# Attention into a bilinear feed-forward layer: query transposes on VectorE, scores in 32-row tiles, folds over eight tiles, and two batches woven together at the start

## The chip, the cores and the metric

The kernel runs on one core of a Trainium2 chip. A core has a matrix engine (TensorE, PE in the profile, with its weight loads shown as PEld), a vector engine (VectorE, DVE), a scalar engine (ScalarE, ACT), GpSimd (POOL), which here mostly issues input transfers, and SyncE (SP), which here issues the output transfers. Each engine runs its own instructions in order; they wait for each other through semaphores. TensorE writes its results to PSUM, a small memory of eight banks per partition, from which VectorE or ScalarE copy them out ("eviction"). The metric is device time in microseconds, the median of several runs.

## The reference

Eight batches of eight heads, 576 positions, head size 64, 32 memory slots per head; then a bilinear feed-forward layer over the 4608 tokens (512 wide, 1536 hidden).

```python
a = np.exp(phi); a = a / a.sum(axis=2)                 # softmax over the 32 slots
k_m = np.einsum('bhsm,bhsd->bhmd', a, k)               # 32 x 64 per head
v_m = np.einsum('bhsm,bhsd->bhmd', a, v)
scores = (q @ k_m.T) / sqrt(64)
attn = softmax(scores, axis=-1)                        # over the 32 slots
x = concat_heads(attn @ v_m)                           # 4608 x 512
out = ((x @ w_a) * (x @ w_b)) @ w_out                  # 4608 x 512
```

## The kernel before

The kernel never forms `x`. For each batch the generator `attention(b)` does, in this order: the exponential of `phi` on ScalarE (`exp_sb`, two instructions); the sums over positions with keys and values (`pkv`, 72 small matmuls, four tiles of the array abreast), copied out as `kvm` with the reciprocals `rphi`; the queries turned by TensorE (`pqT`, 20 transposes) and copied out by VectorE (`qT`); the sums turned (`pT`, 8 transposes) and copied out by ScalarE (`kvT`); the scores (`pscore`, four groups of four matmuls) and their exponential `E` on ScalarE; the denominators (`pD`) with reciprocals `rD` on VectorE; those spread back over the slots (`pR`) and multiplied into `E`, which gives `A`; and the **fold**: the values times the weights, `pva`, in 12 groups of four matmuls, evicted alternately by ScalarE and VectorE into `vab`, the weights of the feed-forward layer for this batch. The weights come in three chunks of 512 columns (`load_wab(n)`), and the fold of chunk n needs chunk n.

`up(b, ...)` then makes the hidden layer of a batch in 12 steps. A step has two halves: four matmuls `pa` (two PSUM tiles of 288 columns, evicted by ScalarE as `a_sb`) and four `pb` (multiplied with `a_sb` by VectorE into `ht`). `down(c)` makes 128 output rows from 12 matmuls `po`, evicted by VectorE or ScalarE in turn (`o_sb`) and stored by SyncE.

The order of the instructions on each engine is the order in which the Python code issues them; there is no scheduler. After every half step `advance` issues a few matmuls of `down` ("work": 48 or 60 in a batch) and then a few yields of the attention of the next batch ("side", 40 spread over the 12 steps, of which the attention uses up 32 or so). The attention of batch 0 runs alone, ahead of the first step:

```python
gens = {b: attention(b) for b in range(1)}
for _ in gens[0]:
    pass
```

The pool `ps_at` has **two** PSUM buffers, taken in turn by everything in the attention (`pkv`, `pqT`, `pT`, `pscore`, `pD`, `pR`, `pva`); `ps_up` has two for `pa` and two for `pb`, `ps_dn` two for `po`. Input transfers stand in one queue on GpSimd, in the order of the calls: batch 0, weight chunk 0, chunks 1 and 2, batch 1, `w_out`, and then one batch per `up`.

Of the kernel before, what the change touches and what calls it, by code (L numbers as in the profile page):

```python
# [13 lines left out]
P = 128  # L14
CS = 16.0
# [3 lines left out]
def kernel(  # L19
# [54 lines left out]
    inputs = {}  # L74
    kv_sbs = [consts.tile([P, 3, NHP, NI * D], F16, name=f"kv_sb{t}") for t in range(2)]
    for t in range(2):
        nc.vector.memset(kv_sbs[t][:, 2], 8.0)

    def load_kv(b):
        phi_sb = inp.tile([P, NHP, NI * M], F32, name="phi_sb")  # L80
        nc.gpsimd.dma_start(out=phi_sb, in_=rows(phi, b))  # L81
        kv_sb = kv_sbs[b % 2]
        nc.gpsimd.dma_start(out=kv_sb[:, 0], in_=rows(k, b))
        nc.gpsimd.dma_start(out=kv_sb[:, 1], in_=rows(v, b))
        inputs[b] = [phi_sb, kv_sb]

    def load_q(b):
        q_sb = inp.tile([P, NHP, NI * D], F16, name="q_sb")
        nc.gpsimd.dma_start(out=q_sb, in_=rows(q, b))
        inputs[b].append(q_sb)  # L90
# [10 lines left out]
    load_kv(0)  # L101
    load_q(0)
# [12 lines left out]
    spread = consts.tile([P, P], F16, name="spread")  # L115
    nc.vector.memset(spread, 0.0)
    for t in range(4):
        nc.gpsimd.affine_select(out=spread, in_=spread, compare_op=ALU.not_equal, fill=8.0 * CS,
                                base=-32 * t, pattern=[[-8, 4], [0, 32]], channel_multiplier=1)
    load_wab(1)  # L120
    load_wab(2)
    load_kv(1)
    load_q(1)
# [6 lines left out]
    def attention(b):  # L130
        phi_sb, kv_sb, q_sb = inputs.pop(b)
        exp_sb = mid.tile([P, NHP, NI, M], F16, name="exp_sb")
        for z in range(2):
            nc.scalar.activation(  # L134
                out=exp_sb[:, 2 * z:2 * z + 2, :, :],
                in_=phi_sb[:, 2 * z:2 * z + 2, :].rearrange("p c (i m) -> p c i m", m=M),
                func=AF.Exp,
            )
            yield

        qT = mid.tile([P, NHP, 5, P], F16, name="qT")
        kvm = mid.tile([P, 2, P], F16, name="kvm")
        kvT = mid.tile([P, 2, 2, P], F16, name="kvT")
        rphi = small.tile([P, 2], F32, name="rphi")

        def transposes(hps, cs):
            t = ps_at.tile([P, len(hps), len(cs), P], F16, name="pqT", tag="at")
            w = min(P, NI * D - P * cs[0])
            for x, hp in enumerate(hps):
                for y, c in enumerate(cs):  # L150
                    nc.tensor.transpose(out=t[:w, x, y, :], in_=q_sb[:, hp, P * c:P * c + w], identity=ident)  # L151
            return t

        pkv = ps_at.tile([P, 2, 3 * D], F32, name="pkv", tag="at")
        for g in range(2):
            for i in range(NI):
                for j in range(4):
                    r, hp = j % 2, 2 * g + j // 2
                    nc.tensor.matmul(  # L159
                        pkv[32 * j:32 * j + 32, g, :],  # L160
                        exp_sb[64 * r:64 * r + 64, hp, i, :],
                        kv_sb[64 * r:64 * r + 64, :, hp, D * i:D * (i + 1)],
                        start=(i == 0),
                        stop=(i == NI - 1),
                        tile_position=(64 * r, 32 * j),
                    )
                if i in (4,):
                    yield
            if g == 0:
                yield  # L170
        nc.vector.tensor_copy(out=kvm, in_=pkv[:, :, 0:2 * D])
        nc.vector.reciprocal(out=rphi, in_=pkv[:, :, 2 * D])
        yield

        for hps, cs in (((0, 1), (0, 1, 2, 3)), ((2, 3), (0, 1, 2, 3)), ((0, 1, 2, 3), (4,))):
            t = transposes(hps, cs)
            w = 64 if cs[0] == 4 else P
            nc.vector.tensor_copy(out=qT[:w, hps[0]:hps[-1] + 1, cs[0]:cs[-1] + 1, :], in_=t[:w])
            yield

        pT = ps_at.tile([P, 2, 2, P], F16, name="pT", tag="at")
        for g in range(2):
            for x in range(2):
                for z in range(2):
                    nc.tensor.transpose(out=pT[64 * z:64 * z + 64, g, x, :], in_=kvm[:, g, D * x:D * (x + 1)],
                                        identity=ident, tile_position=(0, 64 * z))
        nc.scalar.copy(out=kvT, in_=pT)
        yield

        E = mid.tile([P, 2, 640], F16, name="E")  # L190
        Ev = E.rearrange("p g (c two s) -> p g c two s", two=2, s=64)
        for g in range(2):
            for par in range(2):
                n = 5 - par
                ps = ps_at.tile([P, 5, 64], F32, name="pscore", tag="at")
                for j in range(4):
                    h = 4 * g + j
                    nc.tensor.matmul(  # L198
                        ps[32 * j:32 * j + 32, 0:n, :],
                        kvT[64 * par:64 * par + 64, g, 0, M * j:M * j + M],  # L200
                        qT[64 * par:64 * par + 64, h // 2, 0:n, 64 * (h % 2):64 * (h % 2) + 64],
                        start=True,
                        stop=True,
                        tile_position=(64 * par, 32 * j),
                    )
                nc.scalar.activation(out=Ev[:, g, 0:n, par, :], in_=ps[:, 0:n, :], func=AF.Exp,  # L206
                                     scale=rphi[:, g:g + 1])
                yield

        pD = ps_at.tile([P, HALF], F32, name="pD", tag="at")  # L210
        for g in range(2):
            for hf in range(2):
                t = 2 * g + hf
                nc.tensor.matmul(pD[32 * t:32 * t + 32, :], sel, E[:, g, HALF * hf:HALF * (hf + 1)],  # L214
                                 start=True, stop=True, tile_position=(0, 32 * t))
        rD = mid.tile([P, HALF], F16, name="rD")
        for z in range(2):
            sl = slice(z * HALF // 2, (z + 1) * HALF // 2)
            with nc.allow_low_precision("softmax denominators"):
                nc.vector.reciprocal(out=rD[:, sl], in_=pD[:, sl])  # L220
        yield

        A = mid.tile([P, 2, S], F16, name="A")
        for g in range(2):
            for hf in range(2):
                t = 2 * g + hf
                pR = ps_at.tile([P, HALF], F32, name="pR", tag="at")
                nc.tensor.matmul(pR, spread[32 * t:32 * t + 32, :], rD[32 * t:32 * t + 32, :],  # L228
                                 start=True, stop=True, tile_position=(32 * t, 0))
                sl = slice(HALF * hf, HALF * (hf + 1))  # L230
                nc.vector.scalar_tensor_tensor(out=A[:, g, sl], in0=E[:, g, sl], scalar=rphi[:, g:g + 1],  # L231
                                               in1=pR, op0=ALU.mult, op1=ALU.mult)
                yield
        attn[b] = A

        vab = [mid.tile([P, 2, d_ff], F16, name=f"vab{z}") for z in range(2)]
        vabs[b] = vab
        e = 0
        for n in range(NCH):
            for z in range(2):  # L240
                for g in range(2):
                    pva = ps_at.tile([P, 512], F32, name="pva", tag="at")
                    for j in range(4):
                        r, hp = j % 2, 2 * g + j // 2
                        nc.tensor.matmul(  # L245
                            pva[32 * j:32 * j + 32, :],
                            kvT[64 * r:64 * r + 64, g, 1, M * j:M * j + M],
                            w_sbs[z][64 * r:64 * r + 64, hp, 512 * n:512 * (n + 1)],
                            start=True,
                            stop=True,  # L250
                            tile_position=(64 * r, 32 * j),
                        )
                    dst = vab[z][:, g, 512 * n:512 * (n + 1)]
                    if e % 2:
                        nc.vector.tensor_copy(out=dst, in_=pva)  # L255
                    else:
                        nc.scalar.copy(out=dst, in_=pva)  # L257
                    e += 1
                    yield
# [24 lines left out]
    def chain(gens):  # L284
        for g in gens:
            yield from g

    def pump(gen, n):
        for _ in range(n):
            if next(gen, "end") == "end":  # L290
                return False
        return True
# [92 lines left out]
```

## Time and profile before

| what | value |
|---|---|
| median of 3 runs | 322.86 us (321.48 to 323.45) |
| profiled execution | 323.5 us, of it span 321.8 us |
| PE busy | 285.2 us (89%) |
| DVE busy | 170.0 us (53%) |
| ACT busy | 131.3 us (41%) |
| first matmul | at 12.02 us |
| first step of `up(0)` | at 33.03 us |
| last `po` ends, then eviction and store | at 317.3 us |

Times in the trace count from the start of the span. A row of the timeline gives the start, the duration, engine, line, operation, result<-inputs and a count, and in brackets how long the engine was idle before it and who ended that wait. In the chain of work that ended last, a row gives the start, the time until the next piece, and the engine with its result; there a busy TensorE's groups add up to the elapsed time, so these are the rows from which a group's cost is read. A matmul's tile stands ahead of its shape: `64*32` uses 64 rows and 32 columns of the array, `128*128` all of it. The granted clock of TensorE stands in tenths of full speed on the page and as a fraction in the table by windows.

### The profile page before, as it was taken

What the parts mean: (1) busy time and instruction counts of PE and PEld (TensorE: products, weight loads), DVE (VectorE), ACT (ScalarE), POOL (GpSimd) and SP (SyncE); (2) the same over time, 40 slices, a digit from 0 to 9 for tenths busy, and PEclk for the clock granted to TensorE, in tenths of its full rate; (3) what the DMA queues carried; (4) which work ended last, traced back from release to release, by engine and by line L of the source; (5) the groups of instructions that cost most, each with busy time, mean ns of one, the idle gap of its engine ahead of it and who ended that gap; (6) DMA issues with size and microseconds to landing.
All of it is one profiled execution on the core that took longest, in us unless ns stands there. A gap on an engine that the chain in (4) does not pass through costs nothing.

```text
span 321.8 us, 6497 instructions
## 1 busy us (share of the span) xinstructions
PE 285.2 (89%) x2576; PEld 147.5 (46%) x2576; DVE 170.0 (53%) x350; ACT 131.3 (41%) x315; POOL 33.0 (10%) x53
## 2 busy tenths in 40 slices
PE   0438697999899989999899989999899989999994
PEld 0411352365336634455345634465346534566641
DVE  5145256755765466634675547544864565654410
ACT  3023433555364334445345253546264335344300
POOL 8522220002000300012000300000000000000000
PEclk9985587899999999999799999999999999999999
DMA  7999999948612692149512691111102111112144
GB/s 152 204 206 244 207 242 213 241 86 171 134 31 60 138 199 51 27 125 166 100 30 49 135 219 42 40 45 35 32 19 50 35 28 41 33 36 65 35 99 98
DMA packets 24367, 33.46 MB, mean 104 GB/s; under 512 B 1808, under 2 KB 18704, under 8 KB 24336
## 3 DMA queue, kind: packets, MB, share of 16 engines
q0 software_dynamic: 18576, 23.60, 39.8%
q1 hardware_dynamic: 5760, 9.44, 12.2%
q8 instruction: 20, 0.33, 0.4%
q14 instruction: 11, 0.09, 0.1%
HBM read 42.47 MB, written 9.44 MB: 161 GB/s over the span
## 4 chain that ended last, share of the span: by engine, by line
PE 78%; DMA 10%; DVE 5%; ACT 3%; issue 3%; POOL 1%; DVEq 0%; POOLq 0%
PE po L270 27%; PE pb L326 17%; PE pa L317 15%; PE pva L245 8%; DMA kv_sb<-in_v_dram 6%; PE pkv L159 4%; DMA wa_sb<-in_moe_w_a_dram 4%; PE pqT L151 2%; DVE rD L220 2%; PE pR L228 2%; ACT E L206 1%; ACT a_sb L320 1%; PE pscore L198 1%; DVE ht L329 1%; DVE o_sb L276 1%
## 5 line engine op out<-in xcount | busy, mean ns | idle before, releaser
L270 PE MATMUL po<-wo_sb,ht 128*128 128x512 f16 x432 | 121.1, 380 | 0.0
L329 DVE TENSOR_TENSOR ht<-a_sb,pb 128x288 f16<-128x288 f16 x192 | 78.1, 446 | 59.9 <-PE pb L326 55.1
L320 ACT CAST a_sb<-pa 128x288 f16<-128x288 f32 x192 | 67.8, 405 | 80.0 <-PE pa L317 79.6
L326 PE MATMUL pb<-A,vab 128*128 128x288 f16 x384 | 65.8, 295 | 0.1
L317 PE MATMUL pa<-A,vab 128*128 128x288 f16 x384 | 65.6, 295 | 0.0
L270 PEld LDWEIGHTS <-ht 128*128 128x128 f16 x432 | 42.4, 98 | 19.8
L255 DVE CAST vab<-pva 128x512 f16<-128x512 f32 x48 | 33.2, 691 | 33.4 <-PE pva L245 33.1
L257 ACT CAST vab<-pva 128x512 f16<-128x512 f32 x48 | 28.2, 587 | 48.7 <-PE pva L245 48.7
L326 PEld LDWEIGHTS <-vab 128*128 128x128 f16 x384 | 33.4, 100 | 27.8 <-issue 12.6
L317 PEld LDWEIGHTS <-vab 128*128 128x128 f16 x384 | 32.9, 99 | 27.6 <-issue 12.7
L159 PE MATMUL pkv<-kv_sb,exp_sb 64*32 64x192 f16 x576 | 18.4, 270 | 14.4 <-DMA kv_sb<-in_v_dram 14.4
L220 DVE RECIPROCAL rD<-pD 128x144 f16<-128x144 f32 x16 | 15.8, 1026 | 19.5 <-PE pD L214 19.5
L159 PEld LDWEIGHTS <-exp_sb 64*32 64x32 f16 x576 | 12.9, 102 | 23.5 <-issue 20.9
L245 PEld LDWEIGHTS <-kvT 64*32 64x32 f16 x384 | 7.8, 91 | 28.2 <-issue 27.3
L278 ACT ACTIVATE o_sb<-po 128x512 f32<-128x512 f32 x18 | 10.8, 599 | 23.2 <-PE po L270 23.2
L245 PE MATMUL pva<-wb_sb,kvT 64*32 64x512 f16 x192 | 19.4, 420 | 0.9 <-DVE vab L255 0.3
L245 PE MATMUL pva<-wa_sb,kvT 64*32 64x512 f16 x192 | 19.2, 419 | 0.7 <-DVE A L231 0.2
L276 DVE TENSOR_SCALAR o_sb<-po 128x512 f32<-128x512 f32 x18 | 12.3, 686 | 12.0 <-PE po L270 11.9
L231 DVE SCALAR_TENSOR_TENSOR A<-E,rphi,pR 128x288 f16<-128x288 f16 x32 | 15.6, 509 | 4.7 <-PE pR L228 4.5
L206 ACT ACTIVATE E<-pscore,rphi 128x320 f16<-128x320 f32 (+1 forms) x32 | 15.3, 507 | 6.5 <-PE pscore L198 6.0
L228 PE MATMUL pR<-rD,spread 32*128 32x288 f16 x32 | 8.6, 327 | 10.2 <-DVE rD L220 9.2
L81 POOL DMA_DIRECT2D phi_sb<-in_phi_dram x8 | 6.2, 771 | 110.9 <-ACT exp_sb L134 105.1
(33 smaller groups left out, 113.7 us busy)
## 6 DMA issues: line engine op xcount, KB each, us to landing
out_dram<-o_sb SPq DMA_DIRECT2D x72, 128.0 KB, 2.4
phi_sb<-in_phi_dram POOLq DMA_DIRECT2D x8, 576.0 KB, 4.4
kv_sb<-in_k_dram POOLq DMA_DIRECT2D x8, 576.0 KB, 6.6
kv_sb<-in_v_dram POOLq DMA_DIRECT2D x8, 576.0 KB, 9.3
q_sb<-in_q_dram POOLq DMA_DIRECT2D x8, 576.0 KB, 10.5
wa_sb<-in_moe_w_a_dram POOLq DMA_DIRECT2D x3, 512.0 KB, 14.3
wb_sb<-in_moe_w_b_dram POOLq DMA_DIRECT2D x3, 512.0 KB, 16.0
wo_sb<-in_moe_w_out_dram POOLq DMA_DIRECT2D x3, 512.0 KB, 19.8
```

The costliest lines, as they stand in the source:

```text
L159: nc.tensor.matmul(pkv[32 * j:32 * j + 32, g, :], exp_sb[64 * r:64 * r + 64, hp, i, :], kv_sb[64 * r:64 * r + 64, :, hp, D * i:D * (i + 1) ...
L206: nc.scalar.activation(out=Ev[:, g, 0:n, par, :], in_=ps[:, 0:n, :], func=AF.Exp, scale=rphi[:, g:g + 1])
L220: nc.vector.reciprocal(out=rD[:, sl], in_=pD[:, sl])
L231: nc.vector.scalar_tensor_tensor(out=A[:, g, sl], in0=E[:, g, sl], scalar=rphi[:, g:g + 1], in1=pR, op0=ALU.mult, op1=ALU.mult)
L245: nc.tensor.matmul(pva[32 * j:32 * j + 32, :], kvT[64 * r:64 * r + 64, g, 1, M * j:M * j + M], w_sbs[z][64 * r:64 * r + 64, hp, 512 * n:51 ...
L255: nc.vector.tensor_copy(out=dst, in_=pva)
L257: nc.scalar.copy(out=dst, in_=pva)
L270: nc.tensor.matmul(po, ht[:, i, P * c:P * (c + 1)], wo_sb[:, i, :], start=(i == 0), stop=(i == NFF - 1))
L317: nc.tensor.matmul(pa, vab[0][:, g, fs], A[:, g, HALF * hf:HALF * (hf + 1)], start=(g == 0), stop=(g == 1))
L320: nc.scalar.copy(out=a_sb, in_=pa)
L326: nc.tensor.matmul(pb, vab[1][:, g, fs], A[:, g, HALF * hf:HALF * (hf + 1)], start=(g == 0), stop=(g == 1))
L329: nc.vector.tensor_tensor(out=ht[:, i, t0:t0 + HALF], in0=a_sbs[hf], in1=pb, op=ALU.mult)
```

## The change

Five things change together.

1. **Queries.** VectorE transposes the queries itself, SBUF to SBUF, in blocks of 32x32 (four instructions of 576 columns per batch). The 20 TensorE transposes and three copies are gone.
2. **Scores.** Since the blocks put 32 values of the head dimension on 32 partitions, a score is two accumulating matmuls over 32 rows each (`32*32` tiles): 32 matmuls per batch in two units of 16, in place of 16. The turned keys need 16 small transposes for that (and 4 for the values), in place of 8 in all; `kvT` is copied by VectorE in one go.
3. **Sums and fold over eight tiles.** `head(g, j)` swaps the row half for the second group of heads, so that groups g=0 and g=1 use different tiles of the array. A fold unit takes both `ps_at` buffers and issues eight matmuls, alternating between them; ScalarE evicts one, VectorE the other. `pkv` likewise has two buffers, one for each g.
4. **Spread.** `spread` is a full 128x128 matrix for each of the four cases.
5. **Order.** The attention is 18 named units of a batch instead of a generator. Batches 0 to 2 are ordered by hand: only weight chunk 0 is folded ahead of the first steps, the loads of batch 1 go ahead of chunks 1 and 2, the attention of batch 1 runs after four steps of batch 0, with no step beside it up to `dn`, and the steps of batches 0 and 1 alternate as chunks are folded. Batch 2's last seven units run with no step and no `down` beside them. From batch 2 on the 18 units are spread over all 24 half steps, and `down` gets 5.2 matmuls per step as long as there are any.

```diff
-        for hps, cs in (((0, 1), (0, 1, 2, 3)), ((2, 3), (0, 1, 2, 3)), ((0, 1, 2, 3), (4,))):
-            t = transposes(hps, cs)
-            w = 64 if cs[0] == 4 else P
-            nc.vector.tensor_copy(out=qT[:w, hps[0]:hps[-1] + 1, cs[0]:cs[-1] + 1, :], in_=t[:w])
+        def q_transpose(z):
+            for hp in (2 * z, 2 * z + 1):
+                nc.vector.transpose(out=t["qT"][:, hp, :], in_=qs[b][:, hp, :])
...
+    def head(g, j):
+        jj = j ^ g
+        return jj % 2, 2 * g + jj // 2
...
+        def kv_sums(z):
+            if z == 0:
+                t["pkv"] = [ps_at.tile([P, 3 * D], F32, name="pkv", tag="at") for _ in range(2)]
+            for i in ((0, 1, 2, 3, 4), (5, 6, 7, 8))[z]:
+                for g in range(2):
+                    for j in range(4):
+                        r, hp = head(g, j)
...
+        def scores(g):
+            pss = [ps_at.tile([P, NI, 32], F32, name="pscore", tag="at") for _ in range(2)]
+            for dh in range(2):
+                for z in range(2):
+                    for j in range(4):
+                        r, hp = head(g, j)
+                        row = 64 * r + 32 * z
+                        nc.tensor.matmul(
+                            pss[z][32 * j:32 * j + 32, :, :],
+                            t["kvT"][row:row + 32, 2 * g + dh, M * j:M * j + M],
+                            qTv[row:row + 32, hp, :, dh, :],
+                            start=(dh == 0),
+                            stop=(dh == 1),
+                            tile_position=(row, 32 * j),
+                        )
...
+        def fold(n, z):
+            pvas = [ps_at.tile([P, 512], F32, name="pva", tag="at") for _ in range(2)]
+            for j in range(4):
+                for g in range(2):
+                    r, hp = head(g, j)
                     nc.tensor.matmul(
+                        pvas[g][32 * j:32 * j + 32, :],
+                        t["kvT"][64 * r:64 * r + 64, 4 + g, M * j:M * j + M],
+                        w_sbs[z][64 * r:64 * r + 64, hp, sl],
                         tile_position=(64 * r, 32 * j),
                     )
+            nc.scalar.copy(out=vabs[b][z][:, 0, sl], in_=pvas[0])
+            nc.vector.tensor_copy(out=vabs[b][z][:, 1, sl], in_=pvas[1])
...
+    run(0, "exp0 exp1 kv0 kv1 kvt qt0 qt1 sc0 sc1 dn va0a va0b nr0 nr1")
+    ups(steps(0, 0, 4))
+    load(2)
+    run(1, "exp0 exp1 kv0 kv1 kvt qt0 qt1 va0a va0b sc0 sc1")
+    run(0, "va1a va1b")
+    run(1, "dn")
+    ups(steps(0, 4, 6), named(1, "- - nr0 nr1"))
+    ups(steps(1, 0, 4) + steps(0, 6, 8), named(1, "va1a va1b"))
+    run(0, "va2a va2b")
+    ups(steps(1, 4, 8) + steps(0, 8, 12), named(1, "va2a va2b") + named(2, "exp0 exp1 kv0 kv1"))
+    work.ready((S * 1) // P)
+    load(3)
+    ups(steps(1, 8, 12), named(2, "qt0 kvt qt1 - sc0 va0a sc1 va0b"), 5.2)
+    work.ready((S * 2) // P)
+    run(2, "dn va1a va1b nr0 nr1 va2a va2b")
+    every = "exp0 exp1 kv0 kv1 qt0 kvt qt1 va0a sc0 va0b sc1 va1a dn va1b va2a nr0 nr1 va2b"
+    for b in range(2, B):
+        ups(steps(b, 0, NFF), named(b + 1, every) if b + 1 < B else (), 5.2)
```

In the names, `qt` is the query transpose, `kvt` the transposes of the sums, `sc` the scores, `dn` the denominators, `nr` the multiplication into `A`, and `va1b` the fold of chunk 1 with `w_b`.

Two places show what this does to the order on VectorE. The first is the start, the attention of batch 1 (`vab_305`, `vab_306` before and `vab_301`, `vab_302` after are the folded weights of batch 0; `vab_530`, `vab_531` those of batch 1). Before, from the last folds of batch 0 on:

```order
L255 CAST vab_305<-pva 128x512
L255 CAST vab_306<-pva 128x512
L329 TENSOR_TENSOR ht<-a_sb,pb 128x288 x4
L171 CAST kvm<-pkv 128x256
L172 RECIPROCAL rphi<-pkv 128x2
L178 COPY qT<-pqT 128x2x512 x2
L329 TENSOR_TENSOR ht<-a_sb,pb 128x288 x2
L178 COPY qT<-pqT 64x4x128
L329 TENSOR_TENSOR ht<-a_sb,pb 128x288 x2
L220 RECIPROCAL rD<-pD 128x144 x2
```

And after the change, from the first four steps of batch 0 on:

```order
L340 TENSOR_TENSOR ht<-a_sb,pb 128x288 x8
L169 CAST kvm<-pkv 128x128
L170 RECIPROCAL rphi<-pkv 128x1
L169 CAST kvm<-pkv 128x128
L170 RECIPROCAL rphi<-pkv 128x1
L186 COPY kvT<-pT 128x768
L148 STREAM_TRANSPOSE qT<-q_sb 128x576 x4
L252 CAST vab_530<-pva 128x512
L252 CAST vab_531<-pva 128x512
L252 CAST vab_301<-pva 128x512
L252 CAST vab_302<-pva 128x512
L222 RECIPROCAL rD<-pD 128x144 x2
```

Steps of batch 0 (`ht`) stood between the pieces of batch 1's attention; now the whole of it up to `rD` follows in one piece, with two folds of batch 0 in it.

The second place is one batch of the steady part, on VectorE as well. Before, from the sums to the multiplication into `A`:

```order
L171 CAST kvm<-pkv 128x256
L172 RECIPROCAL rphi<-pkv 128x2
L178 COPY qT<-pqT 128x2x512 x2
L329 TENSOR_TENSOR ht<-a_sb,pb 128x288 x2
L178 COPY qT<-pqT 64x4x128
L329 TENSOR_TENSOR ht<-a_sb,pb 128x288 x2
L220 RECIPROCAL rD<-pD 128x144 x2
L329 TENSOR_TENSOR ht<-a_sb,pb 128x288 x2
L276 TENSOR_SCALAR o_sb<-po 128x512
L231 SCALAR_TENSOR_TENSOR A<-E,rphi,pR 128x288 x3
L329 TENSOR_TENSOR ht<-a_sb,pb 128x288 x2
L231 SCALAR_TENSOR_TENSOR A<-E,rphi,pR 128x288
```

After, from the second pair of transposes to the third fold's eviction (`vab_2171` and `vab_2172` are the two halves, for `w_a` and `w_b`, of the next batch's folded weights):

```order
L148 STREAM_TRANSPOSE qT<-q_sb 128x576 x2
L252 CAST vab_2171<-pva 128x512
L340 TENSOR_TENSOR ht<-a_sb,pb 128x288 x4
L252 CAST vab_2172<-pva 128x512
L285 TENSOR_SCALAR o_sb<-po 128x512
L340 TENSOR_TENSOR ht<-a_sb,pb 128x288 x2
L252 CAST vab_2171<-pva 128x512
L340 TENSOR_TENSOR ht<-a_sb,pb 128x288 x2
L222 RECIPROCAL rD<-pD 128x144 x2
L252 CAST vab_2172<-pva 128x512
L340 TENSOR_TENSOR ht<-a_sb,pb 128x288 x2
L252 CAST vab_2171<-pva 128x512
```

Three fold evictions stand ahead of the reciprocals now and two right behind them, where all of them came after `A` before; the transposes take the place of the copies from PSUM.

More of the change, by code (lines that the diff above doesn't have):

```diff
@@ L128, with units, exp_phi @@
     vabs = {}
[L130 to L133, printed above, removed]
+    def head(g, j):
+        jj = j ^ g
+        return jj % 2, 2 * g + jj // 2
+    def units(b):
+        u = {}
+        t = {}
+        def exp_phi(z):
+            if z == 0:
+                t["exp"] = mid.tile([P, NHP, NI, M], F16, name="exp_sb")
             nc.scalar.activation(
-                out=exp_sb[:, 2 * z:2 * z + 2, :, :],
-                in_=phi_sb[:, 2 * z:2 * z + 2, :].rearrange("p c (i m) -> p c i m", m=M),
+                out=t["exp"][:, 2 * z:2 * z + 2, :, :],
+                in_=phis[b][:, 2 * z:2 * z + 2, :].rearrange("p c (i m) -> p c i m", m=M),
@@ L137, in attention @@
                 func=AF.Exp,
             )
[L139 to L164, printed above, removed]
+        def q_transpose(z):
+            if z == 0:
+                t["qT"] = mid.tile([P, NHP, NI * D], F16, name="qT")
+            for hp in (2 * z, 2 * z + 1):
+                nc.vector.transpose(out=t["qT"][:, hp, :], in_=qs[b][:, hp, :])
@@ new lines, in denominators @@
+        def denominators():
+            pD = ps_at.tile([P, HALF], F32, name="pD", tag="at")
+            for g in range(2):
+                for hf in range(2):
+                    x = 2 * g + hf
+                    nc.tensor.matmul(pD[32 * x:32 * x + 32, :], sel, t["E"][:, g, HALF * hf:HALF * (hf + 1)],
+                                     start=True, stop=True, tile_position=(0, 32 * x))
+            t["rD"] = mid.tile([P, HALF], F16, name="rD")
+            for z in range(2):
+                sl = slice(z * HALF // 2, (z + 1) * HALF // 2)
+                with nc.allow_low_precision("softmax denominators"):
+                    nc.vector.reciprocal(out=t["rD"][:, sl], in_=pD[:, sl])
@@ L181, in attention @@
[L181 to L208, printed above, removed]
@@ L221, in attention @@
[L221 to L233, printed above, removed]
@@ L261 @@
+        u["dn"] = one(denominators)
+        u["-"] = lambda: None
+        return u
     hts = {}
@@ L282, in down, with __init__, ready, advance @@
         yield
[L284 to L292, printed above, removed]
-    def up(b, side, work, side_rate, work_rate):
-        A, vab = attn.pop(b), vabs.pop(b)
-        if b % 2 == 0:
+    class Work:
+        def __init__(self):
+            self.gens = []
+            self.next = 0
+            self.owed = 0.0
+        def ready(self, upto):
+            while self.next < upto:
+                self.gens.append(down(self.next))
+                self.next += 1
+        def advance(self, x):
+            self.owed += x
+            while self.owed >= 1.0 and self.gens:
+                self.owed -= 1.0
+                if next(self.gens[0], "end") == "end":
+                    self.gens.pop(0)
+                    self.owed += 1.0
+            if not self.gens:
+                self.owed = 0.0
@@ L352 @@
-    for c in range(next_chunk, T // P):
-        for _ in down(c):
-            pass
+        fs = slice(P * i, P * (i + 1))
+        a_sbs = []
+        for hf in range(2):
+            pa = ps_up.tile([P, HALF], F32, name="pa")
+            for g in range(2):
+                nc.tensor.matmul(pa, vab[0][:, g, fs], A[:, g, HALF * hf:HALF * (hf + 1)],
+                                 start=(g == 0), stop=(g == 1))
+            a_sb = apool.tile([P, HALF], F16, name="a_sb")
+            nc.scalar.copy(out=a_sb, in_=pa)
+            a_sbs.append(a_sb)
```

227 lines of the change are left out of this document (115 added, 112 removed).

## The prediction

> **What bounds the kernel now.** I read the page's head and chain first, then the table by windows, then the chain in order of time.
>
> ```profile
> span 321.8 us, 6497 instructions
> PE 285.2 (89%) x2576; PEld 147.5 (46%) x2576; DVE 170.0 (53%) x350; ACT 131.3 (41%) x315; POOL 33.0 (10%) x53
> PE 78%; DMA 10%; DVE 5%; ACT 3%; issue 3%; POOL 1%; DVEq 0%; POOLq 0%
> 24.00:32.00 8.00, 6.87 (x46) 1.33 (x46) 4.29 (x8) 2.93 (x5) 2.23 (x3) 0.50 1.20 244
> 208.00:244.00 36.00, 34.52 (x330) 18.15 (x328) 21.26 (x45) 16.38 (x41) 0.00 (x0) 1.00 0.16 38
> ```
>
> TensorE carries 78% of the chain; in a steady batch (208 to 244 us) it is busy 34.5 of 36 us at full clock, VectorE 21.3, ScalarE 16.4. So from batch 2 on a group that TensorE need not run is time gained, as long as the other two keep up. The start is different: the 10% DMA lie there, and in 24 to 32 us the granted clock is 0.50.
>
> ```profile
> 12.02 3.05 PE L159 MATMUL pkv<-kv_sb,exp_sb 64*32 64x192 f16 x72 [12.02 <-DMA kv_sb<-in_v_dram]
> 33.03 1.14 PE L317 MATMUL pa<-A,vab 128*128 128x288 f16 x4
> 37.49 0.99 PE L159 MATMUL pkv<-kv_sb,exp_sb 64*32 64x192 f16 x20 [2.36 <-DMA kv_sb<-in_v_dram]
> 101.47 0.65 PE L317 MATMUL pa<-A,vab 128*128 128x288 f16 x4
> 282.19 0.49 PE pa L317 x4
> 303.88 13.39 PE po L270 x62
> ```
>
> These rows cut the span: batch 0 alone until 33.0, then a wait for batch 1's values until 37.5; `up(2)` begins at 101.47, `up(7)` at 282.19, and at 303.88 only the rest of `down` is left. The five batches from 101.47 to 282.19 take 180.7 us, 36.1 each. I treat the change in three parts: start, these five, and the end from 282.19, which keeps its groups (`up(7)` has no attention beside it, and 60 `po` are left over in both orders) and so its time.
>
> **The five steady batches.** The chain in order of time gives what each group costs:
>
> ```profile
> 212.93 0.52 PE pkv L159 x20
> 214.48 0.85 PE pkv L159 x36
> 216.36 0.44 PE pkv L159 x16
> 217.40 0.43 PE po L270 x2
> 217.83 0.89 PE pqT L151 x16
> 218.72 0.49 PE pb L326 x4
> 221.24 0.25 PE pscore L198 x4
> 222.51 0.26 PE pscore L198 x8
> 231.21 0.33 PE pva L245 x4
> 231.54 0.60 PE pb L326 x4
> 232.56 0.54 PE pva L245 x8
> ```
>
> `pb` takes 0.60 behind a tiled group and 0.49 otherwise: leaving the tiled mode costs 0.11. `pkv` fits 0.11 + 0.0205 per matmul (0.85 - 0.44 over 20), so entering costs 0.11 too. `po` is 0.215 per matmul.
>
> *Fold.* Four `pva` cost 0.33 + 0.11 = 0.44, eight in a row 0.54 + 0.11 = 0.65; the second four add 0.21, as they use the same tiles again. A batch has four single and four double groups: 4.36 us. Do eight different tiles run abreast? The eight `pscore` say yes: two fours, one on the lower and one on the upper rows, in two buffers, take 0.26 where four take 0.25. So a fold unit costs 0.44, six cost 2.64: **-1.72**. The Trainium skill (TensorEngine Tiling (Array Packing), Restrictions and Gotchas) says that different row tiles cannot access the same PSUM bank at the same time, and in the new fold each buffer is written from both row halves. By that rule a unit would stay at 0.65. But each four of the old `pva` are written from both row halves into one buffer already, and the second four add just the 0.21 of one 512-column stream, so I hold to the rows.
>
> *Sums.* Three groups, 1.81 + 3 x 0.11 = 2.14, become two of 40 and 32: 72 x 0.0205 + 4 x 0.11 = 1.92: **-0.22**. I take no gain from eight tiles here, as nothing shows the rate at which small matmuls with a new weight load each can start beyond 20.5 ns; at best it halves, another -0.74.
>
> *Transposes.*
>
> ```profile
> 183.70 0.30 PE L151 MATMUL pqT<-ident,q_sb 128*64 128x128 f16 x2
> 184.26 0.66 PE L317 MATMUL pa<-A,vab 128*128 128x288 f16 x4
> ```
>
> 16 `pqT` take 0.89, the last four with the eight `pT` 0.56 (183.70 to 184.26), leaving 0.11: 1.56. The new 20 `pT` at the 0.055 of a `pqT` with 0.22 of mode changes: 1.32, **-0.24**. Column tiles that run abreast would save another 0.66; the old `pT`, two tiles wide, show no such gain.
>
> *Scores, denominators, spread.*
>
> ```profile
> 189.03 0.30 PE L214 MATMUL pD<-E,sel 128*32 128x288 f16 x2 [0.45 <-ACT E L206]
> 191.40 0.29 PE L228 MATMUL pR<-rD,spread 32*128 32x288 f16 x1 [0.82 <-DVE rD L220]
> 226.00 1.01 DVE rD L220
> ```
>
> The scores of before cost 0.95 (0.25, 0.26, 0.22 and two exits). A new unit has two passes, each like the eight `pscore` (0.26 - 0.11 = 0.15), plus 0.22: 1.04 for two, **+0.09**. `pD` costs 1.03 now, 0.45 of it the wait for `E`; with two half steps between `sc1` and `dn` that wait goes: 0.46, **-0.57**. `pR` costs 3 x 0.33 + 0.82 of waiting = 1.81. It becomes full-array, 4 x 0.12, without mode changes, and comes four half steps behind `dn`. But the wait for `rD` doesn't go, it moves: `va1b` needs both buffers, one still holds `pD` until two reciprocals of 1.01 are through, and only a half step (about 1.1) lies between. I put 1.0 there: 1.49, **-0.32**.
>
> Sum: 1.72 + 0.22 + 0.24 - 0.09 + 0.57 + 0.32 = 2.98 a batch, 14.9 in five. TensorE waits behind that fold, and with it the half step and `po` queued there, which is why I count the wait in full.
>
> *Can VectorE follow?*
>
> ```profile
> L255 DVE CAST vab<-pva 128x512 f16<-128x512 f32 x48 | 33.2, 691 | 33.4 <-PE pva L245 33.1
> L178 DVE COPY qT<-pqT 128x1024 f16<-128x1024 f16 x16 | 10.4, 686 | 5.4 <-PE pqT L151 5.3
> L178 DVE COPY qT<-pqT 64x512 f16<-64x512 f16 x8 | 3.3, 407 | 0.0
> L171 DVE CAST kvm<-pkv 128x256 f16<-128x256 f32 x8 | 3.4, 424 | 11.4 <-PE pkv L159 11.4
> L220 DVE RECIPROCAL rD<-pD 128x144 f16<-128x144 f32 x16 | 15.8, 1026 | 19.5 <-PE pD L214 19.5
> ```
>
> It loses the copies, 2 x 0.686 + 0.407 = 1.78. The trace has no VectorE transpose. Per column the casts cost (691 - 424)/256 = 1.04 ns, which makes 576 columns 0.76 us; the copy at 1024 columns in 0.686 bounds it below at about 0.4, the reciprocal (1026 for 144 columns) far above at 4.1. I take 0.76, the rate of the most ordinary rows: 3.0 a batch. `kvT` comes from ScalarE, 768 columns at the copy's rate, 0.55, and a second small cast adds 0.3. 21.3 - 1.8 + 3.0 + 0.55 + 0.3 = 23.4 of a period of 33: enough on average. Within a batch the tight stretch is from `kv1` to `va0a`, five half steps: TensorE has about 6.7 there, VectorE 0.9 + 4 x 0.76 + 3 x 0.85 + 0.55 = 7.0. The two `pb` buffers cover that much, and little more. The Trainium skill (VectorE: DVE Perf Modes, The three transpose paths) has 311 ns for 128 columns, which no row here shows; were that proportional, four transposes of 576 would be 5.6 us a batch, an estimate from that page alone.
>
> **`down` is moved.** Batch 1's steps carry 20 `po` instead of 48, so the five batches carry 28 more: 28 x 0.215 = **+6.0** there, taken from the start. Five batches: 180.7 - 14.9 + 6.0 = 171.8.
>
> **The start.**
>
> ```profile
> 20.76 1.97 DVE L220 RECIPROCAL rD<-pD 128x144 f16<-128x144 f32 x2 [3.41 <-PE pD L214]
> 23.39 2.00 DVE L231 SCALAR_TENSOR_TENSOR A<-E,rphi,pR 128x288 f16<-128x288 f16 x4 [0.66 <-PE pR L228]
> 34.50 1.26 ACT L134 ACTIVATE exp_sb<-phi_sb 128x576 f16<-128x576 f32 x2
> 53.17 1.07 PE pb L326 x4
> 55.13 1.08 PE pa L317 x4
> ```
>
> Transfers keep their total and run back to back; only batch 1 goes ahead of weight chunks 1 and 2, so it lands some 10 us sooner, and those chunks at about 32 to 40. Now step by step. *Batch 0:* `A` is complete at 25.4 before. Transposes behind `kvT` add 1.0, two folds with their evictions between `rD` and `pR` add 2.6: `A` at 29.0, and `up(0)` starts there, 4 us earlier. *Four steps* of 2.1 at half clock (1.07 a group, as at 53.17) and 1.0 when warm: 6, to 35. *Batch 1's attention* is bare: exponentials 1.3, sums 1.5 to 1.9, `kvm` 0.9, transposes and `kvT` 1.7, VectorE's query transposes 3.0 with the fold's eviction 0.7 queued behind them, second fold 1.0, two score units 2.5, two folds of batch 0 at 1.1, `pD`: 15 us, to 50, in which TensorE works about 5. *From 50:* 20 steps at 0.98, 6 of wait for `rD` and `A` and half clock, six folds and waits for buffers 4.5, batch 2's units 5, 20 `po` 4.3: to about 88.5. *Batch 2's last units* are bare again: buffer 0.7, `rD` 2.3, two folds 2.1, `pR` and `A` 2.2, two folds 1.3: 8.5, to 97.0. Then three groups at half clock cost 1.7 more (0.58 each, as at 53 to 59 us): 98.7 against 101.5: **-2.8**. Nothing hides these bare stretches; each microsecond more in them counts once. For the sum I allow 92 to 106.
>
> **Sum.** The profiled execution is 323.5, of it 1.7 outside the span: 323.5 - 14.9 + 6.0 - 2.8 = 311.8. It lies 0.6 above the median of 322.86, so **311** on that scale, 3.7% less.
>
> **Rivals.**
>
> *A: packing goes further.* Eight tiles help `pkv` and the small transposes too: (0.74 + 0.66) x 5 = 7, and about 2 in the bare stretches: 302. The Trainium skill (TensorE: Matmul & The Clock Gate, Wait — 56ns, not 53.3ns?) puts the least distance between starts at 25 ns, which would forbid it; `pkv` already runs at 20.5, so it is open. 0.15.
>
> *B: the fold doesn't pack*, so the change doesn't do what it says: 0.21 x 6 x 8 batches = 10: 321. For it: two buffers and two row halves at once is not in the trace; against it the eight `pscore`. 0.10.
>
> *C: VectorE's queue takes part of it back* in the stretches from `kv1` to `va0a` and from `dn` to `va2b`, 1.5 a batch: 318.5. 0.10.
>
> *D: slower, through the transposes.* With t for one of them, the two bare attentions wait 8 x (t - 0.76), and the tight stretch of five batches 20 x (t - 0.76). From t = 1.19 the gain is gone; at 1.36 (two cycles where the casts take one) it costs 28 x 0.6 = 17: 328. For it: the operation is nowhere in the trace; against it every row but the reciprocal. 0.07.
>
> *E: the start is later*, `up(2)` at 105 by longer bare chains: 318 to 320. 0.06.
>
> **Chances and range.** The forecast has 0.52, with 306 to 316 of its own. The range 302 to 320 takes in A, C and most of E. About 1% is what a measurement tells from no change. Faster by over 1% (below 319.6): the forecast, A, most of C, half of E: 0.80. Within 1%: B, the rest: 0.13. Slower: D, 0.07.
>
> **What would show it.** A fold's eight `pva` next to `pa` in 0.33 (B: 0.54); `STREAM_TRANSPOSE` near 0.76 (D: above 1.2); five batches of about 34.4 with 60 `po` each; TensorE waiting about 1 us at `va1b` for `rD`; `up(2)` near 97, with TensorE mostly idle from 35 to 50 and from 88 to 97. Were TensorE's idle time in a steady batch above 3 us, the sum would be wrong in its assumption that TensorE stays the bound.

## The result, and the profile after

The change makes the kernel faster: 302.8 us median (301.2 to 303.1) against 322.4, a ratio of **0.938** (95% interval 0.934 to 0.943). The forecast was 311 with a range of 302 to 320; the sign is right, and the time lies at the lower edge of the range, outside the 306 to 316 of the forecast itself and near rival A (302). The profiled execution took 302.7, its span 301.0.

The head of the page, the chain's shares by engine, and the new operation's group:

```profile
span 301.0 us, 6648 instructions
PE 258.1 (86%) x2640; PEld 137.8 (46%) x2640; DVE 185.2 (62%) x382; ACT 127.9 (43%) x307; POOL 32.8 (11%) x53
PE 81%; DVE 9%; DMA 3%; ACT 3%; issue 1%; POOL 1%; DVEq 0%; POOLq 0%
L148 DVE STREAM_TRANSPOSE qT<-q_sb 128x576 f16<-128x576 f16 x32 | 22.6, 748 | 0.0
```

TensorE lost 27 us of work and still sets the end; VectorE gained 15 and appears in the chain with 9%. A transpose takes 0.75 us, the 0.76 that the forecast took from the casts.

The cuts that the forecast used, from the timeline of TensorE after the change (first `pa` of `up(0)`, of `up(2)` and of `up(7)`, then the `po` that are left):

```profile
28.24 1.33 PE L328 MATMUL pa<-A,vab 128*128 128x288 f16 x4
96.11 1.14 PE L328 MATMUL pa<-A,vab 128*128 128x288 f16 x4
261.05 0.66 PE L328 MATMUL pa<-A,vab 128*128 128x288 f16 x4
283.38 13.11 PE L279 MATMUL po<-wo_sb,ht 128*128 128x512 f16 x60
```

| part | before | forecast | after |
|---|---|---|---|
| start, to the first `pa` of `up(2)` | 101.5 | 97.0 | 96.1 |
| five batches, to `up(7)` | 180.6 | 171.8 + 1.7 at half clock | 164.9 |
| the rest of the span | 39.8 | 39.6 | 40.0 |

(The forecast took `up(7)` of before from the chain, at 282.19; in the timeline it starts at 282.02, so its five batches are 180.6 and not 180.7.) So 8.6 of the 9.1 us by which the forecast was too high lie in the five steady batches. The chain in order of time, in one of them:

```profile
167.89 0.54 PE pkv L157 x40
170.59 0.45 PE pkv L157 x32
173.21 0.34 PE pT L178 x16
173.54 0.23 PE pT L183 x4
178.45 0.37 PE pscore L199 x16
181.19 0.34 PE pva L243 x8
181.53 0.60 PE pa L328 x4
```

Eight `pva` take 0.34 where they took 0.54, as forecast. But `pkv` falls too: 40 in 0.54 and 32 in 0.45, which is 0.011 per matmul where before it was 0.0205. And the 20 transposes take 0.57 in all, where the forecast had 0.055 for each.

The bare stretches, in the table by windows (PE, PEld, DVE, ACT and POOL busy, granted clock, DMA share, GB/s):

```profile
34.20:48.70 14.50, 7.14 (x161) 2.81 (x160) 7.20 (x15) 5.30 (x11) 4.24 (x6) 0.76 1.22 226
86.00:96.10 10.10, 4.97 (x40) 1.50 (x39) 6.61 (x10) 2.34 (x4) 0.00 (x0) 0.68 0.17 40
208.00:244.00 36.00, 34.75 (x374) 18.37 (x372) 25.89 (x54) 16.81 (x41) 0.00 (x0) 1.00 0.18 42
```

From 34 to 49 us and from 86 to 96 TensorE is busy less than half the time, and the clock falls. In a steady stretch VectorE is busy 25.9 of 36 us, up from 21.3.

### The profile page after: what moved, and what is told of

The parts are those of the page before. It is cut to its first block, busy times and chain, and to the rows that moved or that the text cites. A ratio compares the mean times of both kernels' runs of the same rounds, so it can differ in the third digit from the quotient of the medians.

```text
span 301.0 us, 6648 instructions
## 1 busy us (share of the span) xinstructions
PE 258.1 (86%) x2640; PEld 137.8 (46%) x2640; DVE 185.2 (62%) x382; ACT 127.9 (43%) x307; POOL 32.8 (11%) x53
## 4 chain that ended last, share of the span: by engine, by line
PE 81%; DVE 9%; DMA 3%; ACT 3%; issue 1%; POOL 1%; DVEq 0%; POOLq 0%
PE po L279 30%; PE pa L328 17%; PE pb L337 17%; PE pva L243 7%; DVE rD L222 4%; DMA kv_sb<-in_v_dram 3%; PE pkv L157 3%; PE pscore L199 3%; ACT vab L251 2%; PE pR L229 2%; DVE qT L148 1%; DVE A L231 1%; PE pT L178 1%; PE pD L216 1%; DVE ht L340 1%
## 5 line engine op out<-in xcount | busy, mean ns | idle before, releaser
L279 PE MATMUL po<-wo_sb,ht 128*128 128x512 f16 x432 | 118.0, 382 | 0.0
L328 PE MATMUL pa<-A,vab 128*128 128x288 f16 x384 | 66.5, 295 | 0.9 <-DVE A L231 0.8
L337 PEld LDWEIGHTS <-vab 128*128 128x128 f16 x384 | 36.8, 100 | 25.7 <-issue 5.5
L328 PEld LDWEIGHTS <-vab 128*128 128x128 f16 x384 | 33.9, 100 | 24.1 <-issue 10.2
L208 ACT ACTIVATE E<-pscore,rphi 128x288 f16<-128x288 f32 x32 | 14.3, 497 | 20.6 <-PE pscore L199 20.6
L148 DVE STREAM_TRANSPOSE qT<-q_sb 128x576 f16<-128x576 f16 x32 | 22.6, 748 | 0.0
L243 PE MATMUL pva<-wb_sb,kvT 64*32 64x512 f16 x192 | 14.2, 421 | 9.1 <-ACT vab L251 4.2
L157 PE MATMUL pkv<-kv_sb,exp_sb 64*32 64x192 f16 x576 | 9.6, 259 | 14.1 <-DMA kv_sb<-in_v_dram 13.2
L243 PE MATMUL pva<-wa_sb,kvT 64*32 64x512 f16 x192 | 12.6, 413 | 5.3 <-DVE rD L222 3.3
L231 DVE SCALAR_TENSOR_TENSOR A<-E,rphi,pR 128x288 f16<-128x288 f16 x32 | 14.9, 510 | 3.3 <-PE pR L229 2.6
L157 PEld LDWEIGHTS <-exp_sb 64*32 64x32 f16 x576 | 6.4, 96 | 19.2 <-issue 16.2
```

The lines of the kernel that those rows point to most:

```text
L148: nc.vector.transpose(out=t["qT"][:, hp, :], in_=qs[b][:, hp, :])
L157: nc.tensor.matmul(t["pkv"][g][32 * j:32 * j + 32, :], t["exp"][64 * r:64 * r + 64, hp, i, :], kvs[b][64 * r:64 * r + 64, :, hp, D * i:D * ...
L231: nc.vector.scalar_tensor_tensor(out=attn[b][:, g, sl], in0=t["E"][:, g, sl], scalar=t["rphi"][:, g:g + 1], in1=pR, op0=ALU.mult, op1=ALU. ...
L243: nc.tensor.matmul(pvas[g][32 * j:32 * j + 32, :], t["kvT"][64 * r:64 * r + 64, 4 + g, M * j:M * j + M], w_sbs[z][64 * r:64 * r + 64, hp, sl],
L279: nc.tensor.matmul(po, ht[:, i, P * c:P * (c + 1)], wo_sb[:, i, :], start=(i == 0), stop=(i == NFF - 1))
L328: nc.tensor.matmul(pa, vab[0][:, g, fs], A[:, g, HALF * hf:HALF * (hf + 1)], start=(g == 0), stop=(g == 1))
```

## The experiments

Most change one thing in the changed kernel; what the others combine is said with them. Times are medians, ratios are to the kernel before, run on the same chip: the gap, both woven starts and the order alone ran on another chip (before: 321.9) than the other four (before: 322.6), so between these two groups the ratios are to be compared. The marks are starts of the first `pa` of a batch in the timeline.

| kernel | us | ratio (95%) | `up(0)` | `up(2)` | `up(7)` | five batches |
|---|---|---|---|---|---|---|
| before | 322.4 | 1 | 33.0 | 101.5 | 282.0 | 180.6 |
| the change | 302.8 | 0.938 (0.934 to 0.943) | 28.2 | 96.1 | 261.1 | 164.9 |
| same tiles | 318.9 | 0.988 (0.981 to 0.995) | 28.3 | 102.5 | 277.0 | 174.6 |
| TensorE's queries | 306.7 | 0.947 (0.940 to 0.955) | 28.2 | 96.1 | 265.9 | 169.8 |
| transposes doubled | 321.6 | 0.997 (0.992 to 1.001) | 31.7 | 105.9 | 281.4 | 175.5 |
| gap behind `dn` | 297.1 | 0.923 (0.921 to 0.926) | 26.5 | 95.2 | 255.4 | 160.2 |
| plain start | 293.2 | 0.908 (0.901 to 0.914) | 34.3 | 93.2 | 252.3 | 159.2 |
| woven start | 289.5 | 0.900 (0.898 to 0.902) | 26.4 | 88.6 | 247.8 | 159.2 |
| woven start and gap | 284.2 | 0.884 (0.881 to 0.886) | 26.4 | 87.8 | 242.5 | 154.7 |
| order alone, plain start | 311.6 | 0.968 (0.966 to 0.970) | 35.3 | 96.8 | 269.8 | 173.0 |

With the plain and the woven start `up(1)` has 48 `po` beside it, so these five batches hold 28 `po` (6.0 us) fewer than with the change's start, just as they do in the kernel before.

**The tiles.** Do eight tiles abreast carry the gain?

```diff
-        jj = j ^ g
+        jj = j
```

> The changed kernel, but head(g, j) without the swap: both groups of heads use the same four tiles, in the same order of instructions. Theory P (eight tiles abreast carry most of the gain): a fold's eight pva go back from 0.34 to about 0.54, pkv from 0.0103 to 0.0205 per matmul, so a steady batch gains 6 x 0.21 + 0.74 = 2.0; five batches 10, the start 2 to 4 more: 315 to 317 us. Rival (the gain comes from fewer mode changes, the full-array spread and the new order, and the rates of small matmuls are bound by something other than tiles): within 2 of the changed kernel, 301 to 305.

Measured 318.9: theory P, though 1.9 above its 315 to 317. The chain in order of time of this kernel:

```profile
178.06 0.94 PE pkv L157 x40
181.16 0.77 PE pkv L157 x32
187.97 0.55 PE pva L243 x8
188.52 0.60 PE pb L337 x4
```

Same instructions, same buffers, same mode changes; only the row half differs, and `pkv` is back at (0.94 - 0.77)/8 = 0.021 and the fold at 0.55. That is 0.21 x 6 + 0.72 = 2.0 a batch, and the five batches are 9.6 longer. The start adds 6.4, where P had 2 to 4, although batch 0's values landed 1.8 us earlier in this execution than with the change: three batches' sums and folds at 2.0 each are 6.0 already, so that nothing hides them there.

**The queries.** What does VectorE's transpose bring, with the scores over 32 rows and the narrow `pT` that belong to it, the rest of the change left as it is?

```diff
-                nc.vector.transpose(out=t["qT"][:, hp, :], in_=qs[b][:, hp, :])
+                        nc.tensor.transpose(out=pq[:w, x, y, :], in_=qs[b][:, hp, P * c:P * c + w], identity=ident)
+                nc.vector.tensor_copy(out=t["qT"][:w, hps[0]:hps[-1] + 1, cs[0]:cs[-1] + 1, :], in_=pq[:w])
...
-                            tile_position=(row, 32 * j),
+                        tile_position=(64 * par, 32 * j),
```

> The changed kernel with the queries turned by TensorE as before (pqT, copies by VectorE), 64-row scores in four groups and kvT copied by ScalarE; eight tiles for sums and fold, the spread and the order stay. Theory Q (the time goes by TensorE's groups): per batch pqT and the old pT with one mode change cost 1.56 against 0.77, scores 1.06 against 1.0, so 0.85 a batch, about 5 to 7 in all: 307 to 310 us. Rival (VectorE's four transposes of 0.75 give back what TensorE saves): 301 to 304, or less.

Measured 306.7, 3.9 more: 0.3 below Q's 307 to 310, and above the rival's 301 to 304. The chain in order of time shows what comes back:

```profile
174.48 0.45 PE pqT L152 x8
176.06 0.34 PE pT L183 x8
178.57 0.79 PE pqT L152 x12
181.97 0.23 PE pscore L197 x4
```

The five batches are 4.9 longer: 1.5 in the first and 0.7 to 0.9 in each of the others, where Q had 0.85. The first begins with 5.4 us at half clock, against 3.7 with the change, so its 1.5 isn't the queries alone. At the start nothing comes back: `up(2)` begins at 96.1 in both, presumably because in a bare stretch TensorE's transposes and the copies take about as long as VectorE's transposes.

**VectorE's slack.** Is VectorE far from binding, as its 62% might say?

```diff
-                nc.vector.transpose(out=t["qT"][:, hp, :], in_=qs[b][:, hp, :])
+                for _ in range(2):
+                    nc.vector.transpose(out=t["qT"][:, hp, :], in_=qs[b][:, hp, :])
```

> The changed kernel with each of VectorE's query transposes issued twice (same result). Theory V (the stretch from kv1 to va0a is tight on VectorE, and the bare attentions of batches 0 and 1 wait for it): 4 x 0.75 = 3.0 more per batch, of which 6 in the two bare attentions and about 2.5 to 3 in each of five steady batches: 320 to 324 us. Rival (VectorE has slack, 185 of 301 us busy, and the two pb buffers cover it): only the bare 6 show: 307 to 310.

Measured 321.6, 18.8 more: theory V. The timeline of VectorE and, last, of TensorE in a steady batch:

```profile
189.88 3.04 DVE L149 STREAM_TRANSPOSE qT<-q_sb 128x576 f16<-128x576 f16 x4
192.85 0.65 DVE L253 CAST vab<-pva 128x512 f16<-128x512 f32 x1
193.56 0.43 PE L200 MATMUL pscore<-qT,kvT 32*32 32x288 f16 x12 [1.76 <-DVE vab L253]
```

The fold's eviction stands behind the transposes in VectorE's queue, and the scores wait for its buffer. TensorE's waits over the five batches (in all, times, longest) have this as the largest; with the change it isn't among them:

```profile
PE pscore L200 <- DVE vab L253: 6.8, 5, 1.8
```

Of 3.0 us more per batch 2.1 reach the end (10.6 in five batches). That the two `pb` buffers and what slack there is cover the other 0.9 is likely, but not shown. The start takes 9.8, where V had 6: three batches with 3.0 more each are 9.0 already, so that nothing hides them there.

**The start.** Is the hand-made order of batches 0 to 2, with its order of loads, what brings `up(2)` forward?

```diff
-    load(1)
     load_wab(1)
     load_wab(2)
+    load(1)
...
-    run(0, "exp0 exp1 kv0 kv1 kvt qt0 qt1 sc0 sc1 dn va0a va0b nr0 nr1")
-    ups(steps(0, 0, 4))
...
-    for b in range(2, B):
+    run(0, "exp0 exp1 kv0 kv1 kvt qt0 qt1 sc0 sc1 dn va0a va0b nr0 nr1 va1a va1b va2a va2b")
+    for b in range(B):
         if b + 2 < B:
             load(b + 2)
         ups(steps(b, 0, NFF), named(b + 1, every) if b + 1 < B else (), 5.2)
         work.ready((S * (b + 1)) // P)
```

> The changed kernel with the start of before: all three chunks folded ahead of the first step, batch 1 loaded behind chunks 1 and 2, then every batch from 0 on with the units of the next spread over its half steps and down at 5.2. Theory S1 (the bare stretches of the hand-made start cost more than the earlier first step brings): up(0) and up(1) took 33.3 and 35.2 before and lose about 4.3 each by the packing, so up(2) starts near 93 with 48 po done instead of 20: 302.8 - 3 - 6 = 294 us, faster than the changed kernel. Rival S2 (the hand-made start is what took up(2) from 101.5 to 96.1): up(2) back near 101, 306 to 309 us.

Measured 293.2: theory S1, within 1 us. Two `pa` rows of its timeline (`up(0)` and `up(2)`) and the window of `up(0)`:

```profile
34.34 1.14 PE L328 MATMUL pa<-A,vab 128*128 128x288 f16 x4
93.15 0.66 PE L328 MATMUL pa<-A,vab 128*128 128x288 f16 x4
34.30:62.00 27.70, 23.91 (x284) 12.85 (x277) 20.60 (x45) 14.73 (x36) 4.46 (x7) 0.94 1.20 229
```

`up(0)` starts 6.1 us later than with the change, `up(2)` 3.0 earlier, with 28 more `po` done. The hand-made start costs about 9 us against the plain one: it gets the first step early, and then leaves TensorE with nothing beside batch 1's and batch 2's chains of waits. The clock goes with it: over the whole span the granted clock is 0.992 with the plain start and 0.966 with the hand-made one.

**A start that does both.** Only chunk 0 ahead of the first step, batch 1's loads early, but nothing bare. Batch 1 has an empty unit (`-`) behind its `dn`, which the next experiment tries in the later batches:

```diff
     run(0, "exp0 exp1 kv0 kv1 kvt qt0 qt1 sc0 sc1 dn va0a va0b nr0 nr1")
-    ups(steps(0, 0, 4))
     load(2)
...
+    ups(steps(0, 0, 4), named(1, "exp0 exp1 kv0 kv1") + named(0, "va1a va1b") + named(1, "qt0 kvt"))
+    ups(steps(0, 4, 8), named(1, "qt1 va0a") + named(0, "va2a") + named(1, "sc0") + named(0, "va2b") + named(1, "va0b sc1"))
+    ups(steps(0, 8, 12), named(1, "va1a dn - va1b va2a nr0 nr1 va2b"))
+    work.ready(S // P)
-    for b in range(2, B):
+    for b in range(1, B):
...
```

> The changed kernel with another start: only chunk 0 is folded ahead of the first step and batch 1 is loaded ahead of chunks 1 and 2, as in the change, but batch 1's attention and batch 0's remaining folds are spread over the half steps of batch 0, and from batch 1 on every batch is treated alike, with down. Theory S1: up(0) starts at 28 as in the change and 6 us ahead of e3_plain_start (34.3), nothing is bare, up(2) near 88: 287 to 290 us. Rival (batch 0's steps then wait for weight chunks that land at 32 to 40, or for batch 1's units, so that the earlier start is given back): 292 to 295.

Measured 289.5: theory S1. The rival's wait is there but small, in the timeline of this kernel:

```profile
32.83 0.41 PE L243 MATMUL pva<-wa_sb,kvT 64*32 64x512 f16 x8 [0.75 <-DMA wa_sb<-in_moe_w_a_dram]
35.26 0.41 PE L243 MATMUL pva<-wb_sb,kvT 64*32 64x512 f16 x8 [1.43 <-DMA wb_sb<-in_moe_w_b_dram]
```

Chunk 1 is waited for 2.2 us in all. Of the 3.7 us gained over the plain start not all need be the order: batch 0's values landed 2.1 us earlier in this execution. Its first sums, and then those of the plain start, each waiting for that transfer:

```profile
11.37 1.64 PE L157 MATMUL pkv<-kv_sb,exp_sb 64*32 64x192 f16 x72 [11.37 <-DMA kv_sb<-in_v_dram]
```

```profile
13.48 1.64 PE L157 MATMUL pkv<-kv_sb,exp_sb 64*32 64x192 f16 x72 [13.48 <-DMA kv_sb<-in_v_dram]
```

Counted from that landing, `up(2)` begins 77.3 us later with the woven start and 79.7 with the plain one: in these two executions 2.4 of the 4.5 us between them are the order, and the ratios (0.900 and 0.908) put it at 2.6. In the same way `up(0)` begins 1.8 earlier than with the change, but 15.0 us behind the first values in both, as their order is the same up to there. The granted clock over the span is 0.997.

**The wait for `rD`.** In the changed kernel TensorE begins a fold at `va1b` and stops after its first matmul; the row of the other seven:

```profile
189.34 0.41 PE L243 MATMUL pva<-wb_sb,kvT 64*32 64x512 f16 x7 [0.86 <-DVE rD L222]
```

```diff
-    every = "exp0 exp1 kv0 kv1 qt0 kvt qt1 va0a sc0 va0b sc1 va1a dn va1b va2a nr0 nr1 va2b"
+    every = "exp0 exp1 kv0 kv1 qt0 kvt qt1 va0a sc0 va0b sc1 va1a dn - va1b va2a nr0 nr1 va2b"
```

> The changed kernel with one empty unit between dn and va1b, so that two half steps instead of one lie between the denominators and the next user of their buffer. Theory G (TensorE waits at va1b for the reciprocals that hold pD's buffer, 1.1 a batch): five steady batches lose that wait, 4 to 6 us: 297 to 299. Rival (the wait only moves: VectorE is as late for the next unit, nr0 or va2b): 301 to 304.

Measured 297.1: theory G. In the five batches of the change TensorE waits for `rD` 3.1 us in all (five times); with the gap this wait is gone, they lose 4.7, 0.9 each, and the fold behind the gap runs whole:

```profile
153.49 0.41 PE L243 MATMUL pva<-wb_sb,kvT 64*32 64x512 f16 x8
```

Of the 5.7 in all (4.8 by the ratios), 0.9 lies in the start, where the first values also landed earlier in this execution.

**Both together.**

> e5_woven with the empty unit of e4_gap. Theory G: another 5 to 6 off e5_woven, 282 to 285. Rival: within 1 of e5_woven.

Measured **284.2**, theory G again, the best of this study, 0.884 of the kernel before and 6% under the change. Its page and the first `pa` of `up(2)`:

```profile
span 282.5 us, 6648 instructions
PE 253.1 (90%) x2640; PEld 134.8 (48%) x2640; DVE 180.3 (64%) x382; ACT 126.7 (45%) x307; POOL 32.9 (12%) x53
87.81 0.66 PE L328 MATMUL pa<-A,vab 128*128 128x288 f16 x4
```

**The order alone.** The plain start with TensorE's queries and the same tiles: what is left is the order of the units, the full-array spread and the buffers taken in pairs.

> Only the unit order, the spread and the pairs of buffers of the change: the start of e3_plain_start, the queries on TensorE as in e7_tensor_queries, the same four tiles for both groups as in e1_same_tiles. If the parts add up (tiles 16, queries 4, both measured in the changed kernel): 293.2 + 16 + 4 = 313 us, so the order in itself is worth about 9 of the time before. Rival (the order is worth nothing without the tiles, or the parts overlap): 318 to 323.

Measured 311.6, against 313 if the parts add up. In the five batches, which hold as many `po` as before, the order gives 7.5 (180.6 to 173.0), the tiles and the queries the other 13.8 (to 159.2). But 1.5 of the 7.5 is no work of the order: the profiled execution of the kernel before ran 154.9 to 158.3 us at half clock, inside these five batches, and that of the order alone has no such stretch there. A `pa` and a `pb` of that stretch, in the chain of the kernel before, where they take 0.60 at full clock:

```profile
155.27 1.07 PE pa L317 x4
157.55 0.97 PE pb L326 x4
```

Without it the order gives 6.0.

## Why the prediction was right, and where it was off

*TensorE bounds the steady batches, and a group taken away counts in full.* Right. With the plain start, which has as many `po` in the five batches as the kernel before, and without the half clock just named, a batch saves 4.0 (179.1 to 159.2 in five): tiles 1.9 and queries 0.7 to 0.9, each shown by undoing it, and order 1.2, shown by the order alone. The forecast had 2.98.

*Fold, -1.72.* Right: 0.34 + 0.11 a unit against the 0.44 assumed. Rival B is out: two banks written from both row halves at once did not slow it. The rule of the Trainium skill (TensorEngine Tiling (Array Packing), Restrictions and Gotchas) that different row tiles cannot access one PSUM bank at the same time would have kept the unit at 0.65; in this form, with different column groups, the runs do not bear it out.

*Sums, -0.22.* This is the term that was mis-sized. The two groups cost 0.54 + 0.45 + 2 x 0.11 = 1.21, not 1.92: -0.93. I had taken no gain from eight tiles because nothing seemed to show that small matmuls can start faster than every 20.5 ns. The eight `pscore` that carried the fold could have told: with a weight load each, the second four added 0.01 us in all. And so do the starts of the `pkv` themselves. Their first matmuls, in the timeline cut at 212.90 and 212.98 (before), then at 167.85 and 167.95 (after):

```profile
212.86 0.26 PE L159 MATMUL pkv<-kv_sb,exp_sb 64*32 64x192 f16 x4
212.86 0.35 PE L159 MATMUL pkv<-kv_sb,exp_sb 64*32 64x192 f16 x8
```

```profile
167.82 0.28 PE L157 MATMUL pkv<-kv_sb,exp_sb 64*32 64x192 f16 x8
167.82 0.36 PE L157 MATMUL pkv<-kv_sb,exp_sb 64*32 64x192 f16 x16
```

Before, four start within 10 ns and the next four 82 to 92 ns behind them; after, eight start within 24 ns and the next eight 82 to 94 behind. So 20.5 ns was no rate of starts but four tiles' share of 82 ns, and eight share the same time.

*Transposes, -0.24.* Mis-sized in the same way: 0.34 + 0.23 + 0.11 = 0.68 instead of 1.32. The 32-wide ones run abreast, four tiles at a time. That the old `pT`, 64 columns wide, show no gain from two tiles was a misreading: those 12 transposes at 0.055 and 0.11 for entering would be 0.77, and the row has 0.56; with TensorE's queries eight `pT` of that width take 0.34, which is 0.029 each behind 0.11 for entering.

The two terms together are 1.35 a batch, 6.8 of the 8.6 us. The scores (0.96 instead of 1.04) give 0.4. Another 1.5 is the stretch at half clock in the profile before: the forecast counted it into its 180.7 as if it were work, and it didn't come again. Against this, the half clock at the start of `up(2)` cost 1.8 and not 1.7. A `pa` and a `pb` there, which at full clock take 0.60 (the `pa`, behind a fold) and 0.49:

```profile
96.17 1.07 PE pa L328 x4
98.53 0.96 PE pb L337 x4
```

Rival A is what happened in the steady batches: 6.8 where it had 7, and its 0.15 was too little. That the time falls so near its 302 is in part luck, as the 1.5 has nothing to do with packing.

*The wait for `rD` moves to `va1b`, 1.0.* Right, and shown by the gap, which removes 0.9.

*VectorE can follow.* Right, with the price per column right as well: 0.75. Its tight stretch is real: rival D's slope of 28 us per microsecond of transpose gives 21 for 0.75 more, measured 18.8. Scaled in proportion, the 311 ns that the Trainium skill (VectorE: DVE Perf Modes, The three transpose paths) has for 128 columns would be 1.40, an estimate from that page alone; the trace's 0.75 does not agree with it.

*The start, 97.0.* Right in size, 96.1, with the two bare stretches where they were named, but two misses cancel in it. The first matmul waits for batch 0's values, which landed at 13.2 where the kernel before had them at 12.0:

```profile
13.20 1.64 PE L157 MATMUL pkv<-kv_sb,exp_sb 64*32 64x192 f16 x72 [13.20 <-DMA kv_sb<-in_v_dram]
```

Counted from there, `up(2)` begins 82.9 us later, where the forecast has 85.0. Nearly all of these 2.1 lie ahead of `up(0)`, where batch 0's sums alone take 1.64 and took 3.05 before: the start gained about the 2 that rival A had for it, and the later landing hid 1.2 of them. What the forecast didn't do was to compare this start with another under the new unit costs. Its own two terms, -2.8 there and +6.0 of `po` moved out, already said that the start loses; the plain start shows that it loses about 9.

## What to carry to other kernels

When one row of a profile shows that two groups run abreast, use it for every group of that kind, not only for the one that the change is about. An early first step is no gain by itself: count the work that stands beside each chain of waits, and weave the next batch's chain into steps even where its inputs come late. Where a unit that needs both buffers of a pair stands right behind one whose buffer has a slow reader, it waits for that reader; one empty place in the order took this wait away here, 0.9 us a batch. And before a stretch of a profile becomes the base of a sum, look at its granted clock: 3.4 us at half clock put 1.5 into this one.

## What the runs showed of the hardware

Matmuls on 64x32 tiles with 192 columns and a new weight load each started in groups, one group every 82 to 94 ns, as many to a group as tiles were in turn: with eight that is one every 10.3 to 11 ns over 40 in a row, with four every 20.5; the Trainium skill (TensorE: Matmul & The Clock Gate, Wait — 56ns, not 53.3ns?) has about 25 ns as the least distance between starts, which these runs undercut. TensorE transposes of 128x32 on four column tiles took 0.34 us for 16, those of 128x64 on two column tiles 0.34 us for eight, 0.11 of each for entering the tiled mode; without it that is 14 and 29 ns a transpose, where the full-width ones took 55. A VectorE transpose of 128x576 took 0.75 us.
